# Ordering a fused delta-rule attention and two MoE layers by a greedy list scheduler instead of weighted merges

## The chip, the cores and the metric

The kernel runs on one core of one Trainium2 chip. The metric is the device time of one execution in microseconds (us). A core has five engines that run side by side and meet only at semaphores: PE (TensorE, matmul), DVE (VectorE), ACT (ScalarE), POOL (GpSimd) and SP (SyncE, which here only issues DMAs). Each engine takes its instructions strictly in the order in which the program holds them, so the order is a resource of its own: an instruction that waits holds up all that stands behind it on its engine.

## The reference

```python
# _attn_ref: q, k, v (4 batches, 8 heads, 768 steps, 48); beta (4, 8, 768)
k_n = k / (norm(k) + 1e-6)
for t in range(S):
    y[:, :, t] = q[t] @ state                        # state: 48x48 per batch and head
    state = state + beta[t] * outer(k_n[t], v[t] - k_n[t] @ state)
# _moe_ref: x (3072, 384) = y; 1536 hidden
x = (silu(x @ w_gate) * (x @ w_val)) @ w_out
# _moe2_ref: 2048 hidden
h = x @ w_in
out = elu(h) @ w_out2
```

The weights come as 64-bit floats and are decoded on the chip to pairs of fp32r numbers, a high and a low part; every product of the two MoE layers is three matmul passes (high x high, high x low, low x high).

## The kernel before

**Tiling.** The 3072 tokens are 12 groups of 256 (`NB`): group g holds two batches a = 0, 1 and 128 time steps. Its attention is done in chunks of 32 steps, C = 4 of them, all 8 heads at once. The first MoE layer runs on group after group as its input is there; the second one starts when all are through (`h2`, `out2`), and its order is not touched.

**One group's attention.** `norm` and `nkn` normalise k (the squares on POOL in `ain`, sum on DVE, the root on ACT, the rest on DVE). `trans` transposes q and k on PE into `kq`. `gram` forms the 32x32 products (PE into a PSUM bank, DVE out to `gr`). `inversion` inverts the triangular matrices on DVE: four transposes into `ain`, 31 steps of a multiply and an add (L255, L262) and a transpose back (L270); ACT spreads the result to `zt`. `xstep` multiplies by the inverse. `gstep` (four per group: batch a, head parity) needs four PSUM banks at once; ACT copies each bank to `lc`, DVE adds q's part (L308, L309). `chain` carries the state through the four chunks, one after the other: PE, then two DVE adds for each batch (L326). `yall` gives y, `xtr` transposes it and splits it into `xh`, `xl`, the input of the MoE layer; `xh0`/`xl0` and `xh1`/`xl1` are two buffers that groups use in turn.

**The first MoE layer.** For each group and each of 12 blocks f of hidden units there is a *first projection* (18 matmuls, L478, into one of two banks `gv`), SiLU on ACT, a product on DVE, the high part on ACT and the low part on DVE (L504, L505, L356, L359), and two blocks later the *second projection* (nine matmuls, L521, into `acc`).

**PSUM.** `gv` has two banks, `acc` two, and the four `at` banks serve all of attention.

**Decoding the weights.** The 18 weight tiles of the first layer are decoded in the first stretch: on ACT `low` (L400), `sign` (L435), `abs` (L407) and `cast` (L440), on DVE `or` (L425) and `sub` (L444). A block's projections need its tiles decoded. Some of the temporary buffers are `xh1` and `xl1`.

**What sets the order.** The program is written out by `merge`: two lists of closures with weights are interleaved in proportion. `attention(g, nx)` makes the list of group g and of the beginning of group nx, `moe1` that of the MoE blocks, whole lumps of work per entry (a `gram` of all four products, `gv1` with its four follow-up steps). For group 0, ACT, DVE and POOL are held to the order as written (`inorder`); for the rest, a scheduler in the compiler may move instructions between engines' waits. SP's DMA queue follows the order of the calls.

## Time and profile before

| | us |
|---|---|
| time, median of 3 runs (lowest to highest) | 1242.44 (1239.14 to 1244.08) |
| the profiled execution's own time | 1240.22 |
| its span in the trace | 1238.5 |
| PE busy | 1148.1 (93%) |
| DVE busy | 789.2 (64%) |
| ACT busy | 626.9 (51%) |

The span counts from the first instruction to the last; 1.7 us of the execution's time lie around it. A busy PE in this profile is not a PE at its peak: the ends of matmuls are modelled, and a matmul that waits for its bank inside a run of others hides the wait. The trace falls into four stretches: the start, to the first projection of group 0 at 77.1 us; the decode stretch, where the MoE layer waits for weights and for DVE; eleven groups of attention and first layer side by side; and from 783.0 us the last group's MoE and the second layer, 455.5 us to the span's end.

### The profile page before, as it was taken

What the parts mean: (1) busy time and instruction counts of PE and PEld (TensorE: products, weight loads), DVE (VectorE), ACT (ScalarE), POOL (GpSimd) and SP (SyncE); (2) the same over time, 40 slices, a digit from 0 to 9 for tenths busy, and PEclk for the clock granted to TensorE, in tenths of its full rate; (3) what the DMA queues carried; (4) which work ended last, traced back from release to release, by engine and by line L of the source; (5) the groups of instructions that cost most, each with busy time, mean ns of one, the idle gap of its engine ahead of it and who ended that gap; (6) DMA issues with size and microseconds to landing.
All of it is one profiled execution on the core that took longest, in us unless ns stands there. A gap on an engine that the chain in (4) does not pass through costs nothing.

```text
span 1238.5 us, 31273 instructions
## 1 busy us (share of the span) xinstructions
PE 1148.1 (93%) x13086; PEld 1069.0 (86%) x13086; DVE 789.2 (64%) x2731; ACT 626.9 (51%) x1189; POOL 67.4 (5%) x76
## 2 busy tenths in 40 slices
PE   2474998999999999999999999999999999999998
PEld 2464898889899899999989999989899899899897
DVE  6779648768585849586858664549844545454443
ACT  6597634352526262635344433559744545454443
POOL 4000101010101010100000000000000000000000
PEclk9866799799999999999999999999999999999999
DMA  9730020212121110303030100580000101010000
GB/s 291 197 78 1 14 38 4 41 28 28 27 28 39 16 40 15 53 2 53 2 53 2 29 15 2 181 296 26 21 31 1 52 1 51 1 35 1 26 1 26
DMA packets 106813, 57.15 MB, mean 46 GB/s; under 512 B 76944, under 2 KB 101520, under 8 KB 106672
## 3 DMA queue, kind: packets, MB, share of 16 engines
q1 hardware_dynamic: 106672, 55.16, 17.6%
q8 instruction: 102, 1.67, 0.6%
q14 instruction: 39, 0.32, 0.1%
HBM read 45.71 MB, written 9.44 MB: 45 GB/s over the span
## 4 chain that ended last, share of the span: by engine, by line
PE 79%; DVE 12%; ACT 5%; issue 2%; DMA 1%; POOL 1%; SPq 0%; ACTq 0%; DVEq 0%
PE gv L478 21%; PE acc L521 10%; PE acc L573 8%; PE at L573 8%; PE gv L556 8%; PE at L556 8%; PE at L304 5%; PE at L288 3%; DVE z L262 3%; DVE ain L255 3%; PE at L322 3%; PE at L207 2%; PE at L335 1%; PE at L217 1%; DVE tb L505 1%
## 5 line engine op out<-in xcount | busy, mean ns | idle before, releaser
L478 PE MATMUL gv<-xh,w 128*128 128x256 f32 x1728 | 292.9, 292 | 27.8 <-DVE tb L505 23.4
L478 PEld LDWEIGHTS gv<-xh,w 128*128 128x128 f32 x1728 | 243.6, 196 | 34.7 <-DVE tb L505 25.0
L521 PE MATMUL acc<-hb,w 128*128 128x256 f32 x1296 | 187.4, 290 | 2.0 <-ACT y L528 1.6
L521 PEld LDWEIGHTS acc<-hb,w 128*128 128x128 f32 x1296 | 167.7, 194 | 5.8 <-ACT y L528 1.8
L478 PE MATMUL gv<-xl,w 128*128 128x256 f32 x864 | 155.3, 289 | 0.0
L504 ACT ACTIVATE tb<-gv 128x256 f32<-128x256 f32 x144 | 55.2, 384 | 160.7 <-PE gv L478 158.9
L356 ACT CAST hb<-tb 128x256 fp32r<-128x256 f32 x144 | 58.4, 406 | 149.8 <-DVE tb L505 149.6
L505 DVE TENSOR_TENSOR tb<-gv,tb 128x256 f32<-128x256 f32 x144 | 60.5, 421 | 114.9 <-ACT tb L504 114.2
L478 PEld LDWEIGHTS gv<-xl,w 128*128 128x128 f32 x864 | 127.8, 196 | 0.8 <-DVE xl L359 0.2
L255 DVE TENSOR_TENSOR ain<-z,ain 128x60 f32<-128x60 f32 (+32 forms) x696 | 120.3, 205 | 1.6
L262 DVE TENSOR_TENSOR z<-z,ain 128x60 f32<-128x60 f32 (+32 forms) x696 | 119.7, 210 | 1.4
L563 DVE SCALAR_TENSOR_TENSOR hb<-at,hb 128x512 f32<-128x512 f32 x48 | 33.2, 692 | 84.5 <-ACT hb L562 84.5
L563 DVE SCALAR_TENSOR_TENSOR hb<-gv,hb 128x512 f32<-128x512 f32 x48 | 33.2, 691 | 80.6 <-ACT hb L562 80.6
L359 DVE TENSOR_TENSOR hb<-tb,hb 128x256 fp32r<-128x256 f32 x144 | 60.6, 421 | 28.7 <-ACT hb L356 28.3
L304 PE MATMUL at<-gr,R 32*96 32x80 f32 x1472 | 73.0, 270 | 3.3 <-DVE lc L309 2.5
L304 PEld LDWEIGHTS at<-gr,R 32*96 32x96 f32 x1472 | 61.0, 173 | 14.7 <-DVE lc L309 3.0
L560 ACT ACTIVATE hb<-at 128x512 f32<-128x512 f32 x48 | 28.6, 596 | 85.3 <-PE at L556 85.3
L560 ACT ACTIVATE hb<-gv 128x512 f32<-128x512 f32 x48 | 28.6, 596 | 85.0 <-PE gv L556 85.0
L562 ACT ACTIVATE hb<-hb,neg 128x512 f32<-128x512 f32 x96 | 69.4, 723 | 2.8
L288 PE MATMUL at<-R,zt 64*64 64x96 f32 x768 | 42.9, 264 | 29.9 <-ACT zt L200 29.8
L288 PEld LDWEIGHTS at<-R,zt 64*64 64x64 f32 x768 | 39.5, 147 | 32.9 <-ACT zt L200 31.7
L561 ACT ACTIVATE hb<-hb 128x512 f32<-128x512 f32 x96 | 60.7, 632 | 2.6
(193 smaller groups left out, 2120.6 us busy)
## 6 DMA issues: line engine op xcount, KB each, us to landing
w<-in_moe_w_out_dram SPq DMA_DIRECT2D x28, 384.0 KB, 6.0
w<-in_moe_w_in_dram SPq DMA_DIRECT2D x16, 384.0 KB, 5.2
kp<-in_k_dram SPq DMA_DIRECT2D x12, 384.0 KB, 5.5
qp<-in_q_dram SPq DMA_DIRECT2D x12, 384.0 KB, 4.4
w<-in_moe_w_gate_dram SPq DMA_DIRECT2D x12, 384.0 KB, 8.6
w<-in_moe_w_val_dram SPq DMA_DIRECT2D x12, 384.0 KB, 8.6
R<-in_v_dram SPq DMA_DIRECT2D x24, 192.0 KB, 2.9
x2d<-y SPq DMA_DIRECT2D x12, 256.0 KB, 2.1
```

Source lines behind the costliest of these rows:

```text
L255: V.tensor_tensor(out=t, in0=z[:, l:l + 1, x:y].to_broadcast([128, l, y - x]), in1=an[:, l, 0:l].unsqueeze(2).to_broadcast([128, l, y - x] ...
L262: V.tensor_tensor(out=z[:, 0:l, x:y], in0=z[:, 0:l, x:y], in1=t, op=ALU.add)
L288: nc.tensor.matmul(p[r:r + 64, j], lhsT=zt[r:r + 64, 4 * n + j, :], rhs=R[r:r + 64, 4 * n + j, :], start=True, stop=True, skip_group_check ...
L304: nc.tensor.matmul(ps_[c][0:96, s * 80:s * 80 + 80], lhsT=R[t, u, :], rhs=gr[t, u, 0:80], start=True, stop=True, skip_group_check=True)
L478: nc.tensor.matmul(dst, lhsT=wt[:, a_, kk * 128:(kk + 1) * 128], rhs=xx[:, kk, :], start=(n == 0), stop=(n == 3 * KD - 1))
L505: V.tensor_tensor(out=s, in0=p[:, TB:2 * TB], in1=s, op=ALU.mult)
L521: nc.tensor.matmul(o, lhsT=w[:, a_, d * 128:(d + 1) * 128], rhs=hh[:, b_, :], start=(f == 0 and n == 0 and d != 1), stop=(f == F1 - 1 and ...
L556: nc.tensor.matmul(p, lhsT=W[f][:, 0, a_, kk * 128:(kk + 1) * 128], rhs=x2[n][b_][:, kk, :], start=(m == 0), stop=(m == 3 * KD - 1))
L561: A.activation(out=r, in_=r, func=ACTF.Exp, scale=-1.0)
L562: A.activation(out=r, in_=r, func=ACTF.Identity, bias=neg1, scale=1.0)
L563: V.scalar_tensor_tensor(out=r, in0=p, scalar=0.0, in1=r, op0=ALU.max, op1=ALU.add)
L573: nc.tensor.matmul(ob4[t], lhsT=hh[:, b_, t * 128:(t + 1) * 128], rhs=w[:, a_, :], start=(f == 0 and m == 0), stop=(f == F2 - 1 and m == 2))
```

## The change

All of attention and of the first MoE layer up to group 10 is cut into single steps, each on one engine, with a duration written in by hand, and put in order by a greedy rule before anything is emitted. The rule keeps a clock for each engine and a list of free PSUM banks. Among the heads of nine threads (the second part of all attentions; the first part of all; first and second projections; what follows a projection; the decoding of weights, one thread for each temporary; the zeroing of state) it takes the one that can start earliest, plus a bias: -0.3 for the second part of attention (and the first part of group 0), -0.1 for what follows a projection, 0 for the rest, 0.2 and more for decoding. A step may wait for named others. Every step is emitted with PE, ACT, DVE and POOL held to the order chosen. Further, from tile 6 on the sign of the weights is taken on DVE (`and`, L451) and no longer on ACT; the last group and the second layer stay as they were.

```diff
+    def step(eng, us, fn, name=None, after=(), take=None, give=None, loose=False, at=0.0, bias=0.0):
+    LATENCY = 0.12
+    def schedule(threads):
...
+                b = max([s['at'], busy[s['eng']], 0.0 if s['loose'] else
+                         ends[t][0] + (LATENCY if ends[t][1] != s['eng'] else 0.0)] +
+                        [done[a] for a in s['after']])
...
+                if best is None or b + s['bias'] < best[0]:
+                    best = b + s['bias'], t, b, s
...
+            in_order(lambda: s['fn'](*args), list(EN.values()))
...
+    def thread_first(g):
+        p = [('gd', g - 1, a, par, c) for a in range(2) for par in range(2) for c in range(C)] if g else []
...
+        s('ACT', 1.5 if g else 0.25, lambda: norm2(g))
...
+        s('SP', 0.0, lambda: (load_v(g, 0), load_v(g, 1)), after=p, loose=True)
...
+    def thread_second(g):
...
+            s('PE', 0.35, pe, name=('x', g, a), take=('at', 1), loose=True,
+              after=[('ye', g, a)] + x1 + ([('pe', g - 2, F1 - 1)] if g > 1 else []),
...
+    def threads_moe(seq):
...
+            m.append(step('PE', 2.15, lambda b, g=g, f=f: gv_pe(g, f, gvb[b[0]]), name=('pe', g, f),
+                          after=[('xl', g, 0), ('xl', g, 1), ('dec', pair_of(0, f))], take=('gv', 1),
+                          loose=True, bias=0.0))
...
+    def threads_decode():
...
+                if n < NL:
+                    l.append(step('ACT', 1.93, lambda d=d: d('sign'), **b))
+                else:
+                    l.append(step('DVE', 1.03, lambda d=d: d('and'), **b))
...
-        run(inorder([norm_]))
-        for n in range(2, NW - 2):
-            load_w(n, src1(n))
-        run(inorder([tq, (0, lambda: step(0, 'low')), tk, gm, (0, emit_zero2)]))
...
-            l = merge(steps, moe, scale=(ATT if g else ATT0, 1.0))
-            run(l if g else inorder(l))
+        first = thread_first(0)
+        first.insert(4, step('SP', 0.0, lambda: [load_w(n, src1(n)) for n in range(2, NW - 2)],
+                             loose=True))
+        seq = [(g, f) for g in range(NB - 1) for f in range(F1)]
+        z2 = [step('POOL', 8.0, emit_zero2, after=[('kb', 0, 1)], bias=0.2)]
+        schedule([sum([thread_second(g) for g in range(NB)], []),
+                  first + sum([thread_first(g) for g in range(1, NB)], [])] + threads_moe(seq) +
+                 threads_decode() + [z2])
```

**Place 1: SP's DMA queue at the start.** In the list of group 0 the loading of the 14 further weight tiles is put in before `load_v`. Before:

```order
L377 DMA w_3_111<-in_moe_w_val_dram 128x3x256
L163 DMA R<-in_v_dram 128x8x48 x2
L374 DMA w_6_141<-in_moe_w_out_dram 128x768 x2
L377 DMA w_7_144<-in_moe_w_gate_dram 128x3x256
L377 DMA w_7_144<-in_moe_w_val_dram 128x3x256
L377 DMA w_8_147<-in_moe_w_gate_dram 128x3x256
```

Now, at the end of the loads of the weights:

```order
L405 DMA w_17_169<-in_moe_w_out_dram 128x768 x2
L408 DMA w_18_172<-in_moe_w_gate_dram 128x3x256
L408 DMA w_18_172<-in_moe_w_val_dram 128x3x256
L163 DMA R<-in_v_dram 128x8x48 x2
L160 DMA qp<-in_q_dram 128x16x48
L157 DMA kp<-in_k_dram 128x16x48
```

The values of group 0 (`R<-in_v_dram`), which `xstep` reads, moved from ahead of the 14 weight tiles to behind them; q and k of group 1 follow at once.

**Place 2: DVE at the start, while group 0's gsteps run.** `R<-at` is the output of `xstep`, `lc<-` the adds of `gstep`, L171/L444/L425 (now L171/L475/L456) are the sum of squares of the next group's k, `sub` and `or`. Before:

```order
L200 COPY R<-at_88 128x384
L200 COPY R<-at_86 128x384
L425 SCALAR_TENSOR_TENSOR xl_25_428<-xl_25_428,w_6_141 128x768
L309 TENSOR_TENSOR lc_423<-gv_83,kq 48x4x32
L309 TENSOR_TENSOR lc_423<-gv_84,kq 48x4x32
L309 TENSOR_TENSOR lc_423<-acc,kq 48x4x32 x2
```

Now:

```order
L212 COPY R<-at_87 128x384
L212 COPY R<-at_89 128x384
L171 TENSOR_REDUCE sm_76<-ain 128x16
L475 TENSOR_TENSOR w_25_473<-xl_24_330,w_25_473 128x2x384
L475 TENSOR_TENSOR w_27_493<-dt_123,w_27_493 128x2x384
L330 TENSOR_TENSOR lc_475<-at_87,kq 48x4x32
L330 TENSOR_TENSOR lc_475<-at_86,kq 48x4x32
```

The sum of squares of group 1 now stands ahead of group 0's first gstep; before, it came after group 0's input to the MoE layer was made.

**Place 3: DVE in a late group, from the last gstep on.** `l<-at` are the adds of the last gstep, `sv<-` those of the chain, `tb<-gv` and `hb<-tb` follow a first projection, `gr<-at` belongs to the next group's gram, `xl<-at` to this group's input of the MoE layer. Before:

```order
L309 TENSOR_TENSOR l_67_1306<-at_86,kq 48x4x32
L505 TENSOR_TENSOR tb_247_6905<-gv_84,tb_247_6905 128x256
L326 TENSOR_TENSOR sv<-at_87,st 48x4x48 x2
L359 TENSOR_TENSOR hb_248_6908<-tb_247_6905,hb_248_6908 128x256
L326 TENSOR_TENSOR sv<-at_88,st 48x4x48 x2
L505 TENSOR_TENSOR tb_249_6980<-gv_83,tb_249_6980 128x256
L326 TENSOR_TENSOR sv<-at_89,sv 48x4x48 x2
L359 TENSOR_TENSOR hb_250_6983<-tb_249_6980,hb_250_6983 128x256
L326 TENSOR_TENSOR sv<-at_86,sv 48x4x48 x2
L220 TENSOR_TENSOR gr<-at_87,z_6881 128x4x64
```

Now:

```order
L330 TENSOR_TENSOR l_90_2108<-at_87,kq 48x4x32
L348 TENSOR_TENSOR sv<-at_88,st 48x4x48 x2
L348 TENSOR_TENSOR sv<-at_86,st 48x4x48 x2
L348 TENSOR_TENSOR sv<-at_87,sv 48x4x48 x2
L348 TENSOR_TENSOR sv<-at_88,sv 48x4x48 x2
L348 TENSOR_TENSOR sv<-at_89,sv 48x4x48 x2
L348 TENSOR_TENSOR sv<-at_87,sv 48x4x48 x2
L382 TENSOR_TENSOR xl_326_9181<-at_87,xh_325_9180 128x3x128
L382 TENSOR_TENSOR xl_326_9181<-at_89,xh_325_9180 128x3x128
```

The rounds of the chain followed projections one for one; now they stand in a row with none between them, the group's input to the MoE layer comes right behind, and the next group's gram after that instead of inside the chain.

## Rows read from the trace of the kernel before

**Rows 1.** PE's first projections: start, us, line, tiles, count, [idle before].

```profile
77.10 1.22 PE L478 MATMUL gv<-xh,w 128*128 128x256 f32 x4 [3.40 <-ACT xh L356]
...
494.56 0.62 PE L478 MATMUL gv<-xh,w 128*128 128x256 f32 x3
...
782.97 0.40 PE L478 MATMUL gv<-xh,w 128*128 128x256 f32 x2
```

**Rows 2.** Stretches: length, busy by engine (instructions), granted clock, DMA share, GB/s.

```profile
60.00:140.00 80.00, 50.91 (x633) 46.61 (x633) 63.59 (x204) 68.40 (x88) 6.76 (x6) 0.65 0.13 31
216.00:229.00 13.00, 13.00 (x145) 11.29 (x145) 5.94 (x19) 5.73 (x15) 1.57 (x2) 0.50 0.27 54
440.00:500.00 60.00, 60.00 (x972) 57.22 (x972) 43.53 (x195) 27.11 (x65) 4.70 (x5) 1.00 0.14 28
```

**Rows 3.** One later group on PE, in order of time.

```profile
440.06 2.86 PE L288 MATMUL at<-R,zt 64*64 64x96 f32 x64
...
445.19 0.92 PE L304 MATMUL at<-gr,R 32*96 32x80 f32 x32
...
459.74 1.03 PE L207 MATMUL at<-ident,qp 128*128 128x128 f32 x8
...
465.85 1.73 PE L217 MATMUL at<-kq 48*32 48x64 f32 x128
...
475.22 0.23 PE L335 MATMUL at<-st,lc 96*32 96x48 f32 x1
...
476.72 0.56 PE L322 MATMUL at<-sv,lc 96*48 96x48 f32 x16
...
477.58 0.63 PE L478 MATMUL gv<-xh,w 128*128 128x256 f32 x3
...
480.92 0.52 PE L478 MATMUL gv<-xh,w 128*128 128x256 f32 x3
...
484.15 0.52 PE L478 MATMUL gv<-xh,w 128*128 128x256 f32 x3
```

**Rows 4.** The start: SP's DMA issues, PE's xstep, POOL's squares of group 1.

```profile
7.06 2.84 SPq L163 DMA_DIRECT2D R<-in_v_dram  x2
...
38.18 0.60 SPq L377 DMA_DIRECT2D w<-in_moe_w_val_dram  x1
...
39.74 5.89 PE L288 MATMUL at<-R,zt 64*64 64x96 f32 x64 [23.91 <-ACT zt L200]
...
51.28 1.48 POOL L170 TENSOR_TENSOR ain<-kp 128x768 f32<-128x768 f32 x1 [10.94 <-DMA kp<-in_k_dram]
```

**Rows 5.** DVE at the start: ends of one inversion, four gstep adds, four chain adds.

```profile
22.39 0.19 DVE L255 TENSOR_TENSOR ain<-z,ain 128x31 f32<-128x31 f32 x1
...
37.93 1.06 DVE L270 STREAM_TRANSPOSE ain<-z 128x512 f32<-128x512 f32 x1
...
51.90 1.25 DVE L309 TENSOR_TENSOR lc<-at,kq 48x128 f32<-48x128 f32 x4 [0.47 <-ACT lc L308]
...
60.09 1.50 DVE L326 TENSOR_TENSOR sv<-at,st 48x192 f32<-48x192 f32 x4
```

**Rows 6.** Groups of instructions by line: count, busy us, mean ns, idle before.

```profile
L425 DVE SCALAR_TENSOR_TENSOR xh<-xh,w 128x768 int32<-128x768 int32 x5 | 4.7, 950 | 0.0
...
L435 ACT ACTIVATE w<-w 128x768 f16<-128x768 f32 x18 | 34.7, 1928 | 0.5
...
L420 DVE TENSOR_SCALAR w<-w 128x768 uint8<-128x768 uint8 x16 | 16.8, 1052 | 1.0 <-ACT w L400 1.0
...
L505 DVE TENSOR_TENSOR tb<-gv,tb 128x256 f32<-128x256 f32 x144 | 60.5, 421 | 114.9 <-ACT tb L504 114.2
```

**Rows 7.** A later gstep's way out: ACT's four copies, DVE's four adds.

```profile
449.08 1.40 ACT L308 COPY lc<-at 96x320 f32<-96x320 f32 x4 [0.39 <-PE at L304]
...
449.53 1.26 DVE L309 TENSOR_TENSOR lc<-at,kq 48x128 f32<-48x128 f32 x4 [1.29 <-ACT lc L308]
```

**Rows 8.** One group of eight transposes on PE at the lower clock.

```profile
224.54 1.97 PE L207 MATMUL at<-ident,qp 128*128 128x128 f32 x8
```

More of the change, by code (lines that the diff above doesn't have):

```diff
@@ new lines, in delta_moe_kernel, with traced, in_order @@
+    last = {}
+    busy = {e: 0.0 for e in EN}
+    busy['SP'] = 0.0
+    done = {}
+    units = {'at': [0.0] * C, 'g0': [0.0] * C, 'gv': [0.0] * len(gvb), 'y': [0.0]}
+    taken = {}
+    def traced():
+        return nc.cur_bb.bb.instructions
+    def in_order(x, engines):
+        with ExitStack() as es:
+            for e in engines:
+                if e in last:
+                    es.enter_context(tc.issue_after(last[e]))
+            n = len(traced())
+            x()
+            for i in traced()[n:]:
+                last[i.engine] = i
@@ new lines, in run, with pinned, wrap, f @@
+    def run(l):
+        for _, x in l:
+            x()
+    def pinned(l):
+        def wrap(x):
+            def f():
+                with ExitStack() as es:
+                    for e in (EN['DVE'], EN['ACT']):
+                        if e in last:
+                            es.enter_context(tc.issue_after(last[e]))
+                    x()
+            return f
+        return [(w, wrap(x)) for w, x in l]
+    def anchor(l):
+        return [(w, lambda x=x: in_order(x, [])) for w, x in l]
@@ L811, in after, with put @@
             return l
-        for g in range(NB):
-            moe = moe1(g, before, after)
-            if g == NB - 1:
-                moe = [y if y[0] < 1.0 else anchor([y])[0] for y in moe]
-            if g == NB - 1:
-                moe.insert(0, (0, lambda: load_x2(0)))
-            steps = tail
-            if g + 1 < NB:
-                body, tail = attention(g + 1, g + 2 if g + 2 < NB else None)
-                steps = steps + body
-            l = merge(steps, moe, scale=(ATT if g else ATT0, 1.0))
-            run(l if g else inorder(l))
+        moe = [(0, lambda: load_x2(0))]
+        def put(j, gf, w, x):
+            n = pair_of(j, gf[1])
+            moe.extend(anchor([(w, lambda: x(*gf))]))
+            if gf[0] == NB - 1 and (j == 0 or gf[1] % 2):
+                moe.extend(after(n))
+        for f in range(F1):
+            put(0, (NB - 1, f), 2.0, gv1)
+            held.append((NB - 1, f))
+            while len(held) > (LAG if f < F1 - 1 else 0):
+                put(1, held.pop(0), 1.0, out1e)
+        run(moe)
         late.sort()
```

545 lines of the change are left out of this document (322 added, 223 removed).

## Prediction

> **What bounds the kernel now.** I read the first projections on PE first, since they divide the time into groups: the first one starts at 77.1 us, group 6's at 494.6 and group 11's at 783.0 [rows 1]. So five late groups take 288.4 us, 57.7 each, and 455.5 us follow to the span's end. That tail (the last group's MoE and the second layer) keeps its code and order. The change can only move the 783.0.
>
> Next, the busy times by stretch. From 60 to 140 us, no engine is full: PE 50.9 of 80 us, DVE 63.6 (80%), ACT 68.4, with a clock of 0.65 [rows 2]. DVE and ACT decode weights there while DVE also makes attention, and PE waits for both. From 440 to 500 PE is busy 60.0 of 60 and DVE 43.5, at clock 1.00: PE is the bound [rows 2]. So an order can win where DVE sets the pace, and in a late group only as much as PE's list is shorter than 57.7.
>
> That list, from one late group in time order: a first and a second projection 3.23 (480.92 to 484.15), xstep 2.86, a gstep 0.92, eight transposes 1.03, the gram 1.73, y 1.50 (475.22 to 476.72), a chunk of the chain 0.86 (476.72 to 477.58) [rows 3]. Twelve pairs are 38.8. Xstep, four gsteps (3.7), 16 transposes (2.1), gram, y and four chunks (3.4) make 15.3, and the input's transposes some 0.6. The sum is 54.7; about 3 us of 57.7 are small waits.
>
> **The start: about nil.** SP's queue: group 0's v was asked for at 7.06 and is now asked for behind the weights, whose last issue is at 38.18 [rows 4]. It can't come before about 42, and by the time the other loads take (k of group 1, next in the queue, reached POOL at 51.28 [rows 4]) 46 at the latest. Xstep started at 39.74 [rows 4], so it starts 4 to 6 us later. Held up behind it: ACT's copies and DVE's, and PE, which has nothing else. Then DVE meets group 1's sum of squares ahead of group 0's first gstep. It needs POOL's squares, 51.28 + 1.48 [rows 4], then about 1 us itself, then ACT's root: gstep copies from about 54.5. Before, gsteps and the chain of group 0 shared DVE with decoding (gstep adds at 51.90, chain adds at 60.09 [rows 5]); now that decoding is done in the waits, and four gsteps and four rounds run bare. I take first projection 76, against 77.1, ±3.
>
> **The decode stretch: a gain of about 36 us at group 6.** What decides is when group 2's input is ready, since after it the MoE no longer lacks weights or inputs for some groups. DVE's new list from group 0's input to group 2's, counted from the order: two inversions of 31 steps, 2 × 15.5 (22.39 to 37.93 [rows 5]) and 2 transposes back, 33.2; 24 `or` and `sub` at 0.95, 22.8 [rows 6]; ten `and` at 1.05 [rows 6], 10.5 (the sign, which costs ACT 1.93 a tile, 12 tiles 23.1 [rows 6]); 32 chain adds at 0.375 and 32 gstep adds at 0.31 [rows 5], 22.0; 30 products and low parts at 0.42 [rows 6], 12.6; some 35 others near 0.45, 16. Sum 117. Without any wait group 2's input comes at 76 + 117 = 193. At the 80% of [rows 2] it is 76 + 146 = 222. I take 205, nearer the lower end: decode steps are single now and fill DVE's waits, and ACT, loaded 68.4 of 80, loses 23.
>
> By the order, 15 first projections precede that input, and group 6's first one is the 73rd. Between stand 57 pairs (184.1) and four attentions (4 × 15.3, and their input transposes): 247.7 us of PE. With 1.3 us of waits for each of four groups, 253. So group 6 starts at 205 + 253 = 458, 36 earlier than before.
>
> **The late groups: 31 us of it given back.** The order emits 72 first projections ahead of group 6's input, and exactly 12 per group from there on. So from group 6 each loop waits for its own input, and no reserve of projections is left to hide attention's waits. Earlier the input is ahead: only 44 projections precede group 4's, of the 48 that need none of it. One loop, by hand:
>
> - Gram 1.7, then nine pairs 29.1: 30.8. DVE's way from the gram to the spread matrices is the same length (four transposes and back about 3, the inversion 15.5, thirteen products and low parts in between about 5, copies and ACT's spread the rest).
> - Xstep 2.9, a second projection 1.1, the first gstep 0.9, two pairs 6.5, the next gstep and a second projection 2: 44.0.
> - Two more gsteps. Each needs four banks, and the banks come free only after ACT's copies and DVE's adds, which end at 450.79 for copies that start at 449.08 [rows 7]: 1.7 after PE. With PE's 0.9 and the handing over, a period of 2.8. Then the last one's way out: the chain starts at 51.1.
> - Three rounds of the chain, each bounded by DVE's four adds at 1.50 [rows 5], with no projection between them, only transposes: 55.7. Then y 1.5, the input's transposes and its high and low part (with nothing beside them but one second projection, a chunk and part of the gram): 58.9. Of the last two pairs' work, one first projection (2.15) comes in here: **61.0**, against 57.7.
>
> From 44 to 51 of that loop, PE works 2 us of 7, and the next 8 us are small matmuls. Such a stretch stands in the trace of before: from 216 to 229, where xstep, gsteps and chain of one group were bunched the same way, PE is busy 13.0 of 13 and the clock is 0.50 [rows 2], 1.2 GHz in place of 2.4; eight transposes take 1.97 [rows 8] against 1.03 [rows 3]. At that level a loop loses at least three rounds × 0.8 (transposes 1.9 against 1.0), y's other 1.5, the gram's 1.7 and some of the first pairs: up to 7, so 68. Between 61 and 68 I take 64, since before's own gaps were often too small to lower the clock.
>
> Five loops: 458 + 5 × 64 = 778, against 783.0: 5 us gained. The last group's MoE stays (±3).
>
> **The sum.** First projection −1, decode stretch −35, late groups +31 (5 × 6.3): −5 against the profiled execution's 1240.2, so 1235 as profiled. The median of the runs is 2.2 higher; with the same difference, **1237**. By what a measurement of this kernel can tell from no change, about 0.5% or 6 us, that is within it.
>
> **Rivals.** *A, the sum above.* A faster first half, nearly all given back; own range 1227 to 1247.
>
> *B, the clock holds.* If late groups run at 2.4 GHz throughout, a loop is 61.0 and group 11 starts at 458 + 305 = 763: 20 earlier, 1222. For it: the clock of 440 to 500 is 1.00 [rows 2] although small matmuls of attention stand there too. Against it: there a projection stands between every two of them. If, besides, DVE runs without waits to group 2 (193, 12 less), 1210.
>
> *C, the clock falls in each late group (slower).* The place is the stretch from the last gsteps to the input's split, where PE waits and then has only small matmuls. The price is up to 7 a loop: 68, so 458 + 340 = 798, 15 later: 1257. It decides from a loop of 65.0 on, (783 − 458)/5. For it: [rows 2] of 216 to 229. With group 2's input at 222 instead of 205 it would be 1274.
>
> The Trainium skill ("TensorE: Matmul & The Clock Gate", section "A second HAM failure mode: psum-queue depth-cycling") tells of a kernel in which PE idles briefly between bursts of matmuls while it cycles through PSUM banks, often enough that the clock swings between its two levels, so that throughput suffers though single matmuls at full clock are as fast as ever. By that rule C is what comes. The trace of before agrees in one place, the clock of 0.50 from 216 to 229 [rows 2], and shows at 440 to 500 [rows 2] that the same matmuls between projections don't bring it about.
>
> *D, it doesn't do what it says.* The order chosen could be lost in the build. The order of the built program shows it is not: rounds stand in a row as planned. The remaining way is that the durations written in by hand are so far off that the engines held to one order wait for each other everywhere. That ends as C does, or worse, and is counted there.
>
> **How the numbers follow.** A 0.45, B 0.30, C with D 0.25. Of A, a third to a half is faster by over 0.5% (below 1236.2), about as much within, and a tenth slower (above 1248.6): 0.20, 0.21, 0.04. B is all faster, C nearly all slower (0.01 within). Faster 0.50, same 0.22, slower 0.28. The range leaves out the tenth of the lowest (B with the shorter DVE list) and of the highest (C with the longer): 1213 to 1265.
>
> **What would show it.** In the profile after: first projections of group 0, 6 and 11 near 76, 458 and 778; a DVE wait near 52 to 54 at the sum of squares of group 1; group 2's input near 205; ACT's sign down to a third of its 18 tiles. In a late group, some 5 us of idle PE at the gsteps, a period of 61 to 68, and a granted clock below 1.00 there: at 1.00 and 61, B; at 0.8 or less and 65 or more, C. I am wrong in the first half if group 6 starts later than 475, which would make the DVE list, or the hold of its order, the failing term; and wrong in the second half if late groups take under 60, which would mean that the waits counted one after the other in fact overlap.

## The result

The changed kernel takes 1253.43 us (median of four runs, 1249.71 to 1254.34); the kernel before, run beside it, 1242.19. The ratio is 1.0087 with a 95% interval of 1.0058 to 1.0116: **slower by some 0.9%**, where the prediction said 1237. The profiled execution is the quickest of its four, 1249.71, with a span of 1248.0 against 1238.5 of before, so the profile shows 9.5 of the 11.2 us by which the medians differ; the rest is in no trace.

Where the time went follows from the first projections on PE, as in [rows 1] (line 478 is now 509). Columns: start, duration in us, engine, line, tiles, shapes, count.

```profile
75.20 0.58 PE L509 MATMUL gv<-xh,w 128*128 128x256 f32 x1
...
191.02 0.28 PE L509 MATMUL gv<-xh,w 128*128 128x256 f32 x1
...
245.00 0.28 PE L509 MATMUL gv<-xh,w 128*128 128x256 f32 x1
...
481.32 0.58 PE L509 MATMUL gv<-xh,w 128*128 128x256 f32 x1
...
793.39 0.62 PE L509 MATMUL gv<-xh,w 128*128 128x256 f32 x3
```

These are the firsts of groups 0, 1, 2, 6 and 11. The same stretches of both kernels, from their stretch views:

| stretch | before, us | after, us | difference |
|---|---|---|---|
| to the first projection | 77.1 | 75.2 | -1.9 |
| groups 0 and 1 | 171.6 | 169.8 | -1.8 |
| groups 2 to 5 | 245.9 | 236.3 | -9.6 |
| groups 6 to 10 | 288.4 | 312.1 | +23.7 |
| last group and second layer | 455.5 | 454.6 | -0.9 |

They sum to the 9.5 us of the spans. The shape is as predicted, a gain first and then a loss, but the gain is 13.3 us at group 6 and not 36, and the loss is 23.7.

The stretch view of after (length, busy time of PE, its weight loads, DVE, ACT, POOL, granted clock, DMA share, GB/s): from the first projection to group 2's input, groups 0 and 1, groups 2 to 5, groups 6 to 10 (the late groups), and inside a late group.

```profile
75.20:214.20 139.00, 96.46 (x1435) 88.92 (x1435) 108.12 (x396) 69.91 (x136) 11.04 (x10) 0.79 0.14 31
75.20:245.00 169.80, 127.26 (x1827) 119.41 (x1827) 135.55 (x543) 77.07 (x154) 11.57 (x11) 0.83 0.13 28
245.00:481.30 236.30, 229.35 (x3562) 217.07 (x3560) 155.06 (x646) 108.12 (x253) 19.22 (x19) 0.99 0.13 27
481.30:793.40 312.10, 303.13 (x4616) 286.45 (x4612) 213.80 (x954) 131.55 (x309) 19.89 (x21) 0.95 0.11 24
...
593.60:600.60 7.00, 6.24 (x98) 5.61 (x100) 3.84 (x13) 2.83 (x8) 0.83 (x1) 0.52 0.15 30
```

The late groups of the kernel before, in the same view:

```profile
495.00:783.00 288.00, 286.59 (x4466) 272.88 (x4465) 192.85 (x832) 127.56 (x307) 18.21 (x20) 1.00 0.12 23
```

The granted clock there is 1.00 before and 0.95 now; the last row of after shows one of five short drops, 0.52, about the lower of the two levels (1.2 of 2.4 GHz). Such drops of 3 to 10 us begin at 478, 532, 594, 659 and 724 us, one near the end of each late attention.

One late group on PE, as in [rows 3]; the last column is PE's idle time just before, and who ended it.

```profile
589.00 0.92 PE L320 MATMUL at<-gr,R 32*96 32x80 f32 x32
589.85 1.33 PE L565 MATMUL acc<-hb,w 128*128 128x256 f32 x9
591.68 1.48 PE L320 MATMUL at<-gr,R 32*96 32x80 f32 x32 [0.50 <-DVE lc L330]
593.84 2.54 PE L320 MATMUL at<-gr,R 32*96 32x80 f32 x32 [0.68 <-DVE dt L330]
596.90 0.88 PE L342 MATMUL at<-st,lc 96*48 96x48 f32 x16 [0.53 <-DVE l L330]
...
598.36 1.12 PE L219 MATMUL at<-ident,qp 128*128 128x128 f32 x4
599.40 0.88 PE L342 MATMUL at<-sv,lc 96*48 96x48 f32 x16
...
607.34 0.63 PE L509 MATMUL gv<-xh,w 128*128 128x256 f32 x3
```

From the gstep at 589.0 to the next projection at 607.3, PE has one second projection and otherwise only small matmuls, with short waits between them. A gstep stretches from 0.92 to 1.48 us at full clock (591.68), where some of its matmuls wait inside it for their banks, and to 2.54 us in the next row, where the clock is down besides. Four transposes take 1.12 us, where eight took 1.03 in [rows 3]. The waits that are visible as idle time are small, 0.5 to 0.7 us each. PE's idle time in the late groups is 9.0 us in all, 1.4 before: 1.5 us more a group, so that some 3 of the 4.7 us that a late group has lost lie inside what counts as busy.

The places can be told apart by measuring from one step's first matmul to the next step's. A late group's first and second projections take 41.3 us before and 41.5 now; all the rest, its attention, takes 16.4 before and 20.9 now. So the whole loss of a late group is in attention's steps.

The decode stretch, by who kept PE waiting (us in total, times, longest), from 75 to 245 us:

```profile
PE gv L509 <- DVE w L475: 31.2, 3, 18.6
```

Line 475 is `sub`, the last step of a tile's decoding. The longest of these waits, from 139 to 157 us, is the time in which DVE goes through one inversion without a break, with the tile's `sub` behind it in the held order. DVE waits too; its longest sums from the first projection to group 2's input, 75.2 to 214.2 us, are for ACT's part behind a projection and a gstep, and for PE's chain:

```profile
DVE tb L540 <- ACT tb L536: 7.9, 8, 1.7
DVE sv L348 <- PE at L342: 5.7, 2, 3.5
DVE hb L550 <- ACT hb L546: 4.1, 5, 1.5
DVE l L330 <- ACT l L324: 3.7, 1, 3.7
```

### The profile page after: what moved, and what is told of

It is laid out like the page before. It is cut to its first block, busy times and chain, and to the rows that moved or that the text cites. A ratio compares the mean times of both kernels' runs of the same rounds, so it can differ in the third digit from the quotient of the medians.

```text
span 1248.0 us, 31369 instructions
## 1 busy us (share of the span) xinstructions
PE 1138.7 (91%) x13086; PEld 1056.1 (85%) x13086; DVE 805.7 (65%) x2743; ACT 611.2 (49%) x1177; POOL 71.3 (6%) x76
## 4 chain that ended last, share of the span: by engine, by line
PE 78%; DVE 11%; DMA 4%; ACT 3%; issue 2%; SPq 1%; POOL 0%; ACTq 0%; DVEq 0%; POOLq 0%
PE gv L509 23%; PE acc L565 11%; PE acc L625 8%; PE at L625 8%; PE at L608 7%; PE gv L608 7%; PE at L342 4%; PE at L320 3%; PE at L308 2%; PE at L219 2%; DVE z L283 2%; DMA w<-in_moe_w_val_dram 2%; DVE ain L276 2%; PE at L231 2%; PE at L356 2%
## 5 line engine op out<-in xcount | busy, mean ns | idle before, releaser
L509 PE MATMUL gv<-xh,w 128*128 128x256 f32 x1728 | 289.1, 291 | 38.9 <-DVE w L475 31.2
L276 DVE TENSOR_TENSOR ain<-z,ain 128x60 f32<-128x60 f32 (+32 forms) x696 | 116.9, 204 | 1.6
L540 DVE TENSOR_TENSOR tb<-gv,tb 128x256 f32<-128x256 f32 x144 | 60.3, 420 | 67.3 <-ACT tb L536 66.2
L550 DVE TENSOR_TENSOR hb<-tb,hb 128x256 fp32r<-128x256 f32 x144 | 70.6, 491 | 29.1 <-ACT hb L546 28.9
L320 PE MATMUL at<-gr,R 32*96 32x80 f32 x1472 | 55.4, 261 | 10.4 <-DVE lc L330 5.9
L308 PE MATMUL at<-R,zt 64*64 64x96 f32 x768 | 36.2, 250 | 30.1 <-ACT w L466 29.7
L320 PEld LDWEIGHTS at<-gr,R 32*96 32x96 f32 x1472 | 47.5, 166 | 17.8 <-DVE dt L330 3.5
L308 PEld LDWEIGHTS at<-R,zt 64*64 64x64 f32 x768 | 33.8, 138 | 32.1 <-ACT w L466 29.9
```

The costliest lines, as they stand in the source:

```text
L276: V.tensor_tensor(out=t, in0=z[:, l:l + 1, x:y].to_broadcast([128, l, y - x]), in1=an[:, l, 0:l].unsqueeze(2).to_broadcast([128, l, y - x] ...
L308: nc.tensor.matmul(p[r:r + 64, j], lhsT=zt[r:r + 64, 4 * n + j, :], rhs=R[r:r + 64, 4 * n + j, :], start=True, stop=True, skip_group_check ...
L320: nc.tensor.matmul(banks[c][0:96, s * 80:s * 80 + 80], lhsT=R[t, u, :], rhs=gr[t, u, 0:80], start=True, stop=True, skip_group_check=True)
L509: nc.tensor.matmul(dst, lhsT=wt[:, a_, kk * 128:(kk + 1) * 128], rhs=xx[:, kk, :], start=(n == 0), stop=(n == 3 * KD - 1))
L550: V.tensor_tensor(out=hh[:, 1, :], in0=gvp.pop((g, f))[1], in1=hh[:, 0, :].bitcast(F32), op=ALU.subtract)
```

## The experiments

Each kernel ran beside the kernel before on the same chip, but not all on one chip: the median of before lay between 1241.4 and 1243.1 us, so rows compare better by their ratios than by their times. Times are medians; "late group" is the mean of groups 6 to 10, from the starts of their first projections in the profiled execution. The kernels with the changed one's order on PE in late groups (e4, e7, e16 but for its small filler) have 62.9 there, against the 62.4 of its quickest execution: a difference of half a microsecond there says nothing.

| run | time, us | ratio to before (95%) | late group, us |
|---|---|---|---|
| before | 1242.19 | 1 | 57.7 |
| changed | 1253.43 | 1.0087 (1.0058 to 1.0116) | 62.4 |
| e4_v_early | 1251.69 | 1.0074 (1.0057 to 1.0092) | 62.9 |
| e7_sign_act | 1246.35 | 1.0034 (1.0018 to 1.0050) | 62.9 |
| e3_decode_first | 1262.34 | 1.0164 (1.0136 to 1.0193) | 62.8 |
| e2_filler | 1258.47 | 1.0132 (1.0115 to 1.0148) | 64.0 |
| e15_filler_small | 1245.92 | 1.0037 (1.0020 to 1.0053) | 61.6 |
| e16_filler_tiny | 1251.55 | 1.0079 (1.0049 to 1.0110) | 62.9 |
| e17_filler_sign | 1240.72 | 0.9991 (0.9976 to 1.0007) | 61.6 |
| e18_filler_sign_all | 1254.27 | 1.0095 (1.0069 to 1.0122) | 61.6 |
| e9_gram_in_chain | 1260.2 | 1.0143 (1.0123 to 1.0164) | 62.1 |
| e10_hold_three | 1263.07 | 1.0179 (1.0149 to 1.0208) | 64.1 |
| e11_both | 1265.66 | 1.0193 (1.0171 to 1.0214) | 62.8 |
| e12_both_sign_act | 1264.31 | 1.0177 (1.0147 to 1.0206) | 62.6 |
| e13_old_pe_order | 1294.04 | 1.0408 (1.0395 to 1.0421) | 65.2 |
| e14_old_pe_order_sign_act | 1294.15 | 1.0405 (1.0381 to 1.0429) | 65.1 |
| e1_ahead | 1344.2 | 1.0825 (1.0803 to 1.0847) | see text |
| e5_gram_ahead | 1355.39 | 1.0906 (1.0866 to 1.0947) | see text |
| e8_decode_loose | 1357.24 | 1.0927 (1.0893 to 1.0962) | see text |
| e6_decode_mixed | 1366.14 | 1.0990 (1.0950 to 1.1030) | see text |

### The start

**v ahead of the weights** (e4_v_early):

```diff
-        first.insert(4, step('SP', 0.0, lambda: [load_w(n, src1(n)) for n in range(2, NW - 2)],
+        first.insert(8, step('SP', 0.0, lambda: [load_w(n, src1(n)) for n in range(2, NW - 2)],
```

> Undoes one part: group 0's v is asked for ahead of the 14 weight tiles again. My prediction's reading: xstep starts near 40 us in place of 45, but the gsteps' copies still wait for the sum of squares of group 1, whose k lands near 51, so that the first projection stays at 75 within 1 us and the total within 3 us. Rival (the late v is what holds the start): the first projection comes 4 to 5 us earlier, and the total is 4 to 5 lower.

PE's waits at the start, of the changed kernel and then of this one:

```profile
44.75 4.32 PE L308 MATMUL at<-R,zt 64*64 64x96 f32 x64 [29.69 <-ACT w L466]
...
54.43 1.84 PE L320 MATMUL at<-gr,R 32*96 32x80 f32 x29 [3.13 <-DVE lc L330]
```

```profile
40.95 5.73 PE L308 MATMUL at<-R,zt 64*64 64x96 f32 x64 [26.99 <-ACT zt L212]
54.65 1.69 PE L320 MATMUL at<-gr,R 32*96 32x80 f32 x25 [5.73 <-DVE lc L330]
```

Xstep comes 3.8 us earlier, and so do the first two gsteps behind it, but the third comes no earlier: PE waits 5.73 in place of 3.13. DVE shows why in the changed kernel: it waits for POOL's squares of group 1, and the adds stand behind that.

```profile
51.49 0.95 DVE L171 TENSOR_REDUCE sm<-ain 128x16 f32<-128x768 f32 x1 [1.83 <-POOL ain L168]
...
54.10 0.87 DVE L330 TENSOR_TENSOR lc<-at,kq 48x128 f32<-48x128 f32 x4
```

This part of the prediction held to the microsecond (first projection 75.7 here, 75.2 there): the late v costs nothing, because of the other wait.

### The decode stretch

**Sign on ACT** (e7_sign_act):

```diff
-    NL = 6
+    NL = 18
```

`NL` is the number of tiles whose sign is taken on ACT.

> The changed kernel with the sign of all 18 tiles on ACT again, as before the change: DVE gets 12.6 us less, ACT 23 us more between 75 and 245 us. If DVE's load is what delays group 1 and 2 there: group 1 starts 5 to 10 us earlier than 191, and group 2's input comes before 210 in place of 214. If ACT's share (it makes the temporaries that `sub` waits for) is: both come later, by up to 10.

The last step of group 2's input on DVE, in the changed kernel and in this one, and this one's stretch from the first projection to group 2's:

```profile
213.65 0.56 DVE L382 TENSOR_TENSOR xl<-at,xh 128x384 fp32r<-128x384 f32 x1 [0.19 <-ACT xh L377]
```

```profile
207.72 0.56 DVE L382 TENSOR_TENSOR xl<-at,xh 128x384 fp32r<-128x384 f32 x1 [1.22 <-ACT xh L377]
```

```profile
76.40:243.40 167.00, 126.48 (x1828) 119.17 (x1828) 126.60 (x532) 95.01 (x166) 12.19 (x11) 0.83 0.13 28
```

Group 2's input is ready at 208.3 in place of 214.2 us, group 6 starts at 476.6 in place of 481.3, and the median is 7 us lower; the traces show 4.7 of it at group 6 and 2.3 at group 11, the changed kernel's being that of its quickest execution. Group 1 starts no earlier (191.9), so that half of the forecast missed. Of the two readings it is DVE's load that counts: from the first projection to group 2, DVE is busy 126.60 us in place of 135.55 and ACT 95.01 in place of 77.07, and the input comes 5.9 us sooner.

**Decoding ahead of attention** (e3_decode_first):

```diff
-    DB = 0.2
+    DB = -0.4
```

> One number changed: the bias of decoding, -0.4 in place of 0.2, so that decode steps go ahead of attention. By the order, group 1's input stands behind 11 first projections in place of 7, and group 2's behind 24 in place of 15: no reserve is built from group 2 on. My theory (in the changed kernel PE stands idle for 29 us at 88 and 139 us because `sub` of a tile stands behind the passes of an inversion): the waits of projections for `sub` fall from 31 us to under 10, group 1 starts near 170 in place of 191. Groups 2 to 5 then run without reserve, about 62 each in place of 59, which gives 12 back: total 4 to 10 below the changed kernel. Rival (DVE is full there, so whatever goes first delays the other): group 1 and 2 start within 5 us of the changed kernel's, total the same or up to 15 above.

Projections wait less for decoding, and group 0 takes 92.4 us in place of 115.8. But decoding now goes ahead of group 0's own attention too, and the first projection comes at 90.4. Group 1 starts 8 us earlier (182.8 for 191.0), but group 2 at 243.9, against 245.0: for group 2 the rival had it, whatever goes first puts off the rest. I had forecast a gain of 4 to 10 us; the total is 9 us higher, and I had not seen that group 0 would pay. Most of the loss comes later: with no reserve of projections built, groups 2 to 5 take 249.6 us in place of 236.3, about the 12 that the expectation had put there.

### The late groups

**The next attention far ahead** (e1_ahead; for groups above 2, -0.6 is below the -0.3 of the chain):

```diff
-        e = -0.3 if g == 0 else 0
+        e = -0.3 if g == 0 else -0.6 if g > 2 else 0
```

> One number changed: from group 3 on the first part of an attention (normalising, transposes, gram, inversion) gets the bias -0.6 in place of 0, so that it goes ahead of the second part of the group before and of projections. By the order, group 6's input then stands behind 60 first projections and not 72: a whole group in reserve, and a projection stands between every two rounds of the chain. The start and the decode stretch are nearly as in the changed kernel (group 1 behind 7 projections, group 2 behind 17 in place of 15). My theory (late groups lose 4.7 us each because the MoE has used up its blocks when attention comes to gsteps and chain): five late groups take 57 to 58.5 us each in place of 62.4, the clock stays 1.00 there, and the total is some 20 us or more below the changed kernel, 1225 to 1233. Rival (the loss lies in single steps held in one order on four engines, whatever that order): late groups stay at 61 or more, total 1245 or more.

It lost 91 us against the changed kernel. Groups 1 and 2 take 85 and 89 us in place of 54 and 59, groups 3 to 8 take 71 to 74; groups 9 and 10 are shorter, 53 and 39, as no further group's attention is begun beside them. Who kept PE waiting from 435 to 720 us, four groups, and what DVE does in one of these waits (its passes of the inversion left out, between 534 and 550):

```profile
PE at L342 <- DVE sv L348: 42.4, 4, 12.2
```

```profile
533.89 0.14 DVE L260 COPY z<-zd 128x32 f32<-128x32 f32 x1
...
549.61 1.06 DVE L291 STREAM_TRANSPOSE ain<-z 128x512 f32<-128x512 f32 x1
550.57 1.47 DVE L348 TENSOR_TENSOR sv<-at,sv 48x192 f32<-48x192 f32 x4
```

A whole inversion stands on DVE ahead of the chain's adds; the chain waits on PE, and behind it wait projections that need none of it. What matters is not how far ahead something is but which long block goes in front of what PE needs next. The rival's numbers came, but for this reason, which neither reading had; the run didn't test my theory, its bias was wrong for that.

**The inversion behind the chain** (e5_gram_ahead):

```diff
+        e = [-0.3 if g == 0 else -0.6 if g > 2 else 0]
...
+        if g > 2:
+            e[0] = -0.2
         for n, x in enumerate(inv[:-4]):
```

> From group 3 on, normalising, transposes and gram of the next group get the bias -0.6 as in the run e1_ahead, but the inversion and the spread get -0.2, behind the chain's adds at -0.3 (in e1_ahead the passes of an inversion stood as a block ahead of two rounds of the chain on DVE, and PE waited 10 to 13 us there in every group). By the order, a projection stands between every two steps of an attention, gram stands inside the chain, and group 6's input is behind 60 first projections, not 72. Theory (the changed kernel's late groups lose by bunched gsteps and rounds without projections to cover them): periods from group 3 on fall to 55 to 58 us, clock 1.00, no wait of PE above 2 us there; group 11 starts near 245 + 9 x 57 = 758, total 1212 to 1225, faster than before. Rival (a held order of four engines is stiff, and each step ahead costs another its wait): periods of 60 and more, total 1240 or more.

The same again at another place. -0.2 is behind the chain, but ahead of the -0.1 of what follows a projection, and now the bank of a projection is not emptied while an inversion runs, from 444 to 737 us:

```profile
PE gv L509 <- DVE tb L540: 50.0, 4, 12.8
```

Two variants of it, e6_decode_mixed with decoding at -0.4 and the early gram from group 1 on, and e8_decode_loose with decoding at -0.1, both with group 0's attention at -1.0, have the same wait (49.2 and 49.7 us in four groups), at 1366.14 and 1357.24 us; what they were to tell of decoding in the total is lost under it. Before it sets in, e8 brings the first projection to 68.7 us, and group 1 still starts at 190.7, no earlier than in the changed kernel.

> As e5_gram_ahead, from group 1 on, and besides: group 0's attention gets the bias -1.0 and decoding -0.4 (in place of 0.2), so that decoding goes ahead of inversions but behind group 0's attention, which it delayed by 15 us in e3_decode_first. If decoding behind the inversion is what PE waits for (31 us in the changed kernel): the first projection stays near 76, group 1 starts at 165 to 180 in place of 191, and the total is 10 to 20 below e5_gram_ahead. If DVE is simply full there: group 1 starts sooner and group 2 later, total within 5 of e5_gram_ahead.

> As e5_gram_ahead, with group 0's attention at -1.0 and decoding at -0.1, between e5_gram_ahead (0.2) and e6_decode_mixed (-0.4). Decoding goes ahead of what has the bias 0, behind inversions from group 3 on only. If the price of decoding first is a later inversion, this run lies between the two in group 1's start and in the total.

**Gram inside the chain, and projections held back** (e9, e10, e11, e12). With the bias of what follows a projection below the inversion's, the order is as wanted:

```diff
-            ma.append(step('DVE', 0.42, lambda g=g, f=f: gv_mul(g, f), bias=-0.1,
+            ma.append(step('DVE', 0.42, lambda g=g, f=f: gv_mul(g, f), bias=-0.4,
...
+        hold = {7: ('gs', 0, 0), 8: ('gs', 0, 1), 9: ('c', 1, 0), 10: ('c', 1, 1), 11: ('c', 1, 2)}
...
-                          after=[('xl', g, 0), ('xl', g, 1), ('dec', pair_of(0, f))], take=('gv', 1),
+                          after=[('xl', g, 0), ('xl', g, 1), ('dec', pair_of(0, f))] +
+                          ([(hold[f][0], g + 1, *hold[f][1:])] if g > 2 and f in hold else []), take=('gv', 1),
-                          loose=True, bias=0.0))
+                          loose=True, bias=-0.6 if g > 2 and f in hold else 0.0))
```

The first change (in all five steps of that thread) with e5's biases is e9, the others alone are e10, all together e11; e12 has the sign on ACT besides, and moves the gram from group 2 on. In all four the products of the gram go two by two, so that two PSUM banks stay for the chain.

> From group 3 on: normalising, transposes and gram of the next group at -0.6 (the four products of the gram two by two, so that two PSUM banks stay for the chain), inversion at -0.2, and what follows a projection at -0.4 in place of -0.1. In e5_gram_ahead, that last bias was behind the inversion's, and the passes of a whole inversion stood ahead of the products of a projection on DVE: PE waited 12.8 us a group for its bank. Here the order has the gram inside the chain, the inversion interleaved with those products, and twelve projections per group with none in reserve (group 6 behind 72). Theory 1 (the gram behind the group's input lengthens the loop): the loop loses the gram, its way out and part of the transposes from its end, 3 to 4 us: late groups take 58 to 60 in place of 62.4. Theory 2 (the bunch of gsteps and chain with no projection between costs it, and stays): late groups stay at 61 to 63, low clock in each.

> The changed kernel with only this: from group 3 on, the last blocks of a group wait, in the plan, for steps of the next group's attention (block 7 and 8 for its first two gsteps, 9, 10 and 11 for its first three rounds of the chain, at the bias -0.6 there), and the gram goes two by two. By the order one projection moves in between two gsteps and one between two rounds, and the others come behind the input of the next group; gram stays behind it. Theory 2 (bunching): late groups fall from 62.4 to 59 to 61, the clock drops get shorter or go. Theory 1 (loop length by the gram): 62 or more, since the projections that are held lengthen the loop.

> e9_gram_in_chain and the holding of e10_hold_three together: by the order two projections stand between the gsteps and three between the rounds of the chain, six during the inversion, and the gram is inside the chain. If both theories hold part of the loss: late groups take 56 to 58, clock 1.00, group 11 starts 25 to 30 us earlier than in the changed kernel, total 1220 to 1232. If PE's own work per group is larger than I count (12 x 3.39 + 16 = 56.7): 58 to 59.5, total 1232 to 1240.

> e11_both from group 2 on, with the sign of all tiles on ACT as in e7_sign_act (7 us below the changed kernel): if the two effects add, 5 to 8 below e11_both.

None of it shortened a late group: 62.1, 64.1, 62.8 and 62.6 us. So neither the gram's place nor the missing projections between the rounds, taken as orders on PE, is a cause that these runs could lift out by itself. The second isn't cleared by this: in e10 another wait came in, for ACT's spread of the inverse, and PE's idle time in the late groups rose from 9.0 to 22.0 us.

```profile
PE at L308 <- ACT zt L212: 14.3, 10, 2.0
```

In e9 and e11 the total is higher for another reason too: with -0.4, the steps that follow a projection go ahead of inversions at the start as well, and group 1 starts at 202 us in place of 191, group 2 at 255 in place of 245.

**The old order on PE** (e13_old_pe_order): the rule may choose a PE step of a late group only if it is next in a list that repeats the order of the kernel before.

```diff
+                while script and script[0] in done:
+                    script.pop(0)
+                if s['name'] in inside and s['name'] != script[0]:
+                    continue
```

> The greedy rule as it is up to group 3; from there on PE's steps must be chosen in the order in which the kernel before had them (a projection behind xstep, one behind every two gsteps, one behind every round of the chain, transposes and gram inside the chain, two blocks in reserve when the next input is made), while DVE, ACT, POOL and SP are still ordered by the rule. If the place of PE's steps among the projections is what costs late groups 4.7 us each: periods from group 3 on are 57.5 to 59.5, clock 1.00, and the 13 us that group 6 was ahead of the kernel before are kept: total 1226 to 1236, faster than before. If the rule's order on DVE and ACT is the cost: periods stay at 61 or more, total 1245 or more.

Besides, from group 5 on the first part of an attention has the bias -0.6 up to the gram, the gram goes two by two, and the last round of the chain goes ahead of the input's transposes, as the list needs it. The periods of groups 3 to 9 are 65 to 73 us. PE's waits from 510 to 779 us:

```profile
PE at L308 <- ACT zt L212: 10.8, 8, 2.0
PE at L320 <- DVE lc L330: 8.7, 7, 2.2
```

PE follows the order that gave 57.7 us, step for step in groups 6 and 7, and now waits for ACT to spread the inverse and for DVE to empty the gsteps' banks. All of the loss lies there: in group 6 the first round of the chain comes 31.1 us after the group's start, in group 7 of the kernel before 21.6, and from there on both take some 37. So the second reading holds here: with PE's order given, what the rule's plan makes of the order on ACT and DVE costs some 7.5 us a group. Whether that is the choice itself or the holding to it wasn't tried apart, and the order on ACT and DVE is not that of the changed kernel. The same with the sign on ACT, from group 2 on (e14_old_pe_order_sign_act), gives 1294.15 us: nothing is added.

> e13_old_pe_order from group 2 on, with the sign of all tiles on ACT. If the 6 us by which e7_sign_act brought group 2's input forward add to it: 3 to 8 below e13_old_pe_order, 1220 to 1232. If DVE's relief is lost in PE's order: equal within 3.

### The clock

**Nine useless matmuls at six places of a late group** (e2_filler). Nobody reads their result.

```diff
+        def fill(k):
+            if g > 6:
+                def pe(b):
+                    for n in range(9):
+                        nc.tensor.matmul(gvb[b[0]][:, 0:TB], lhsT=w1(0, 0)[:, 0, 0:128],
+                                         rhs=xh[(g - 1) % 2][:, n % KD, :], start=(n == 0), stop=(n == 8))
+                s('PE', 1.08, pe, name=('f', g, k), take=('gv', 1), give=(('f', g, k), None), loose=True)
```

> The changed kernel with nine matmuls of a projection's shape, whose result nobody reads, put at six places of each late group (attention of groups 7 to 11): ahead of the last two gsteps, of the three rounds of the chain and of y. It adds work and removes nothing. If the lower clock is what late groups lose most to: the drops at 478, 532, 594, 659 and 724 us go, eight transposes fall from about 1.9 to 1.0, and the five late groups come down from 62.4 us to 60 or less each although 6.5 us of work are added. If bare waits (banks, copies, adds) are it: the clock may rise, but a group takes 62.4 to 64. If there is no room in those waits: 66 or more.

The drops in the late groups after 478 us are gone, and a late group takes 64.0: the middle reading. But it adds some 6.5 us of work to each group, so it can't say what the clock costs. Two smaller fillers do: three matmuls (e15_filler_small), and one of 32 columns (e16_filler_tiny). In the order of PE, DVE and ACT they are the same kernel.

> e2_filler with three matmuls at each place in place of nine: 2.2 us of added work per late group. If the low clock costs a late group something that e2_filler won back and then spent on its own filler: late groups take 61 or less, transposes back to 1.0. If the clock costs nothing on the path: 62.4 to 63.5, whether it is up or not.

> e15_filler_small with one matmul of 32 columns at each place in place of three of 256: the same order on all engines, but nearly no work in the waits. If it is the clock: the drops in late groups are there again, late groups take 62 to 62.6 in place of 61.6, total 1251 to 1254. If it is the order or chance: late groups at 61.6 or less, total 1246 or less.

Group 7 of the changed kernel, of e15 and of e16 (same columns as above):

```profile
544.90:607.30 62.40, 60.17 (x926) 57.17 (x922) 43.63 (x194) 27.33 (x64) 4.84 (x5) 0.95 0.13 27
```

```profile
541.60:603.20 61.60, 60.61 (x945) 57.54 (x941) 43.69 (x194) 27.38 (x64) 4.85 (x5) 1.00 0.14 28
```

```profile
543.70:607.70 64.00, 62.32 (x934) 59.84 (x928) 43.66 (x194) 27.32 (x64) 4.84 (x5) 0.92 0.13 27
```

With three matmuls in each place, the granted clock is 1.00 and the group shorter, though it has more work; with the small one, it is 0.92 and the group is not. What gets shorter is attention's small matmuls, in the late groups of the changed kernel and of e15 (lines: count, busy us, mean ns, idle before):

```profile
L342 PE MATMUL at<-sv,lc 96*48 96x48 f32 x240 | 10.6, 238 | 1.2 <-DVE xl L382 1.2
...
L219 PE MATMUL at<-ident,qp 128*128 128x128 f32 x32 | 8.0, 398 | 0.0
```

```profile
L342 PE MATMUL at<-sv,lc 96*48 96x48 f32 x240 | 8.7, 212 | 1.6 <-DVE xl L382 1.6
...
L219 PE MATMUL at<-ident,qp 128*128 128x128 f32 x32 | 5.3, 287 | 0.0
```

Transposes fall from 398 to 287 ns, chain matmuls from 238 to 212; e16 has 435 and 251. So the low clock costs a late group at least the 1.3 us that e15 has on e16 (62.9 to 61.6), net of its filler, and 5.6 us in the total. The 61.6 lies between the two forecasts of e15 (61 or less, 62.4 or more); e16 came out as its clock reading had it. The Trainium skill ("TensorE: Matmul & The Clock Gate", section "A second HAM failure mode: psum-queue depth-cycling") tells of a clock that swings between its two levels because PE idles briefly between groups of matmuls as it cycles through PSUM banks. The trace agrees: the stretch in which gsteps and chain cycle through four banks with short waits (593.60 to 600.60) is the one at 0.52.

**Both parts together** (e17_filler_sign; e18_filler_sign_all with the filler from group 1 on):

> e15_filler_small (from one group earlier) with the sign of all tiles on ACT as in e7_sign_act. Each alone was 7 us below the changed kernel. If they add: 1238 to 1241, at most 0.3% from the kernel before, and the late groups still take 61 to 62. If both come from the same place: 1244 to 1247.

> e17_filler_sign with the three matmuls in every group from the first one on. In the decode stretch PE waits 10 to 18 us at a time, which 0.36 us can't bridge, so that the clock there stays low: within 2 us of e17_filler_sign.

e17 gives 0.9991 (0.9976 to 1.0007): what the change lost is back, and nothing is won. The two parts add, as forecast. e18 is 13.5 us slower than e17, where I expected no difference: its group 2 starts 4.9 us later (247.4 for 242.5), and its groups 2 to 5 take 240.1 us in place of 232.6, with 54 more useless matmuls (group 5 has its 18 in both). There PE has projections at hand and is the bound, and each useless matmul is paid in full: at the 0.124 us of one in a projection, the 54 come to 6.7 of the 7.5 us.

## Why the prediction was wrong

**The start** was right: -1.9 us at the first projection, for -1. The wait for group 1's sum of squares and the hidden wait for v were both as read.

**The decode stretch** was the failing step: group 6 starts at 481.3 us and not at 458, so that the gain was 13 us and not 36. With late groups 8 us shorter in all than taken (312.1 for 320), group 11 starts at 793.4 and not at 778, and the sign turns. Of the 23.3 us at group 6, 9.2 arose up to group 2's input and 13.4 behind it. The prediction's own sign of being wrong, a group 6 later than 475, was there, but it named only DVE's list or the hold of its order; the larger part is the price of PE's steps. Two terms were mis-sized.

- Group 2's input was put at 205, between 193 and 222, as "decode steps are single now and fill DVE's waits". It came at 214.2. DVE's list was no longer than reckoned, 108.1 us for 117; its waits were the mistake, 31 us where 12 were left for them (108.12 busy of 139.00, 78%, near the 80% of [rows 2]). Single decode steps did not fill them: DVE stood 18.1 us for ACT's copies and what ACT does behind a projection (lines 540, 550, 330) and 6.7 for PE's chain (line 348). PE in turn waited 31.2 us for `sub`, as an inversion, once begun, ran to its end ahead of it, 18.6 us in the longest of these waits. e7 shows that the stretch moves with DVE's load: there DVE is busy 97.5 of the 131.9 us from the first projection to group 2's input, 10.6 less, and the stretch is 7.1 shorter. Decoding first (e3) moved group 2's start by only 1 us, though another order can delay it (e9, e11).
- From there to group 6 I counted 253 us, from a pair of projections at 3.23 and an attention at 15.3 and 0.6. It took 266.4 (214.2 to 480.6, when group 6's input is ready). Measured from one step's first matmul to the next step's, in groups 2 to 5: 48 first projections take 106.8 us and 48 second ones 55.7, 3.39 for a pair; four attentions 73.8, 18.4 each. Over 57 pairs and four attentions that is 9 and 10 us more, and most of the 5 us of waits I had added are inside it. The row of 3.23 was one quiet place. In the late groups of before, too, a pair takes 3.44 and an attention 16.4, and these make up the 57.7: the 3 us "of small waits" that I left over lie inside the steps, where no idle time shows them. They aren't the price of a pair by itself: group 10 of e1_ahead, which has no attention beside it, takes 39.0 us for its twelve pairs, 3.25 each.

**The late groups** went nearly as reckoned. The loop by hand had the chain at 51.1 us and the whole at 61.0. Group 7 (from 544.9) has its chain at 52.0, and the whole, 62.4, lies between the 61 and the 64 taken. The reserve of projections was used up as read from the order. The clock fell in every late group, as rival C said, but by drops of 3 to 10 us; e15 won back 1.3 us a group net of its filler, which itself takes 2.2 by the estimate below, so the cost was some 1.3 to 3.5 us and not 7. C's point of decision was a loop of 65, on the ground that group 6 would start at 458; from 481.3 it is (783.0 - 481.3)/5 = 60.3, and 62.4 lies beyond it. So the sign turned on the first half's size, not on the late groups.

**The sign on DVE** I had entered as a term of DVE's list (10.5 us) without asking what it was worth to keep it off. By e7 it cost the kernel some 7 us, and ACT, which it relieved, was not the bound in the changed kernel: 77 us busy of 169.8.

**What stays open.** With the clock held, a late group takes 61.6 and not 57.7. Of the 3.9 us, the filler itself may take up to 2.2 (an estimate: 18 matmuls at the 0.12 us of one in a projection, 106.8 us for 864). Measured from a step's first matmul to the next step's, the filler's places take 3.6 us a group in e15, attention 17.6 (16.4 before) and the projections 40.5 (41.3 before): so most of what is left stands at the filler, in its work or in waits that it covers. No run here took those waits away; e9 to e13 changed the order five ways and found nothing clearly shorter, and e13 points to the order on ACT and DVE. Why the order of before, which nobody planned step by step, has no such waits isn't shown.

## What to carry to other kernels

Read the price of a step from the mean over many groups, from its start to the next one's, and not from a quiet row: waits inside a busy matmul unit don't show, and here 5% on each pair and 2.5 us on each attention put group 6 back by 13 us net of the waits allowed for, more than the 9.5 us by which the kernel lost. When a planner chooses the order by bias, ask of each long block (an inversion of 116 instructions) what stands behind it on its engine, since in e5 a tenth of a microsecond of bias stood for over 12 us of waiting in each group. Ask also which engine's list the stretch that counts moves with: here the sign moved to DVE, 80% busy there, and that cost some 7 us, though ACT was relieved.

## What the runs showed of the hardware

Work that nobody needs made the kernel faster: 18 matmuls of 256 columns in the waits of each late group brought the granted clock from 0.95 to 1.00 and the total from 1253.43 to 1245.92 us; six matmuls of 32 columns at the same places left it at 0.94 and 1251.55. It paid only where PE would wait: put into groups in which PE is the bound, the same matmuls (54 of them) cost 7.5 us. And a pair of projections took 3.25 us where nothing stood between pairs (group 10 of e1_ahead), but 3.39 to 3.44 in groups with attention between them.
